# Attention beside a feed-forward block on one core: the bounds' minimum taken once, the ranges compared together, a round's parts summed into C, and another table for the planner

## The chip, the cores and the metric

The kernel runs on one core of one Trainium2 chip. Its time is the device time of one execution, in microseconds (us). Five engines work side by side, each through its own list of instructions in order: TensorE (PE in the profile, its weight loads PEld), VectorE (DVE), ScalarE (ACT), GpSimd (POOL) and SyncE (SP), which here issues nearly all transfers. An instruction that waits holds up everything behind it on its own engine. The kernel before takes 1034.79 us (median of three runs, 1033.28 to 1035.25).

## The reference

One input `x` of 2048 rows by 512 columns goes through two branches, and a gate per row mixes them:

```python
x = A_x
g = _sigmoid((x * gate_w).sum(-1, keepdims=True))
a = _A_ref(x, A_wq, A_wk, A_wv, A_wo)   # attention: 32 heads of 16 columns, one shared k and v
b = _B_ref(x, B_w1, B_w2)               # silu(x @ w1) @ w2, 1792 hidden columns
return g * a + (1 - g) * b
```

Attention is `softmax(q k^T / 4) v` for each of 32 heads over all 2048 keys. That is 32 x 2048 x 2048 exponentials, and all of them are taken on ACT.

## The kernel before

**Rounds and steps.** The queries are cut into 4 chunks `c` of 512 rows and 4 groups `o` of 8 heads; a round is half a group (`rb` 0 or 1), so there are 32 rounds. A round has 16 steps `s`, one for each 128 keys, and a step has two halves `p`. For each half PE makes scores `S` for 128 keys of two heads by 512 queries (L1363, 8 small matmuls, two at 64 rows each of the array's height side by side), and ACT takes the exponential of 128x1024 of them into `P` (L1369). That makes 1024 activations, with two score buffers between PE and ACT. Then the sums over the keys: `pv += P v` (L1467).

**Two ways for a step's sums.** `P` is float32. Either PE multiplies it as it is with `VF` (float32; "native", 16 matmuls in the trace for a step in one piece, or 32 narrower ones for a step in two halves), or DVE first subtracts the upper 16 bits of `P` from it into `L` (L1388), and PE multiplies the upper half and `L` with 16-bit `VP` (8 + 8 matmuls). The second way takes less of PE and one DVE subtraction over 128x2048.

**The end of a round.** When a round's last sums are in, DVE transposes the two accumulators into `T` and `U` (L1282, L1283). GpSimd adds them (L1288), scales six "digits" of v by powers of a quarter into `U` (L1289) and adds the two halves of `T` (L1290). DVE sums the digits (L1304), adds them to their base, column 0 of `T` (L1305), takes the reciprocal of the denominators (L1306) and multiplies into `C` (L1309). After two rounds `turned` transposes `C` and splits it into 16-bit `O` (L1315 to L1318) for the output product. In the last round DVE does GpSimd's part too (`late`).

**The work between.** The feed-forward block (`ffn_h`, `ffn_o`), the q products of later blocks and the output products are fed to PE in small slots of four or eight matmuls between scores (`f_slot`, L1009): four when one product uses half of the array's rows, eight when two products share it. What has not been placed when the rounds are over runs at the end as whole 128-row matmuls (L1013). Results are added to `acc` on DVE (L983) and stored.

**The bound of the scores.** The exponential is taken of scores shifted by a bound computed from |q| and the largest |k| (`q_bound`, then `shift` writes `s1`, which SP stores to `sh` in DRAM through `q_shift`, L516). To know at the end that no bound was too loose, `q_shift` returns `note`: the least entry of `s1`, one DVE reduction for each of the 16 blocks into a column of `um` (L518). The planner queues it as a task of low urgency.

**The check.** When all pieces of weights are split, `chores` take largest absolute values of the operands (L254). When those are done and no block's bound is open, `gather` folds `um` and `mxs` into one row (L815 to L819), SP sends that row to DRAM and `row` brings it back to one partition (L820, L825). `check` compares eleven ranges, three at a time, each with a reduction and two comparisons (L831 to L836); `verdict` writes `flag` (L839 to L841). If it is raised, a second pass computes everything again with measured scales.

**What sets the order.** Nothing is scheduled at run time. While the program is written, a planner keeps a clock for each engine (`pe`, `act`, `dve`, `pool`) and writes the instructions in the order its rules choose: `put(dur, ready, due, f)` queues a DVE task, `serve` takes open tasks by their due time, and the main loop decides between scores, sums and slots. `Way` holds twelve thresholds of these rules, and the table `WAYS` gives new values every eight halves `p`. So a changed duration in a `put`, or another row in the table, moves instructions on every engine.

Of the kernel before, what the change touches and what calls it, by code (L numbers as in the profile page):

```python
# [18 lines left out]
SHIFT = 32.0  # L19
# [19 lines left out]
    *[(0.1, 0.3, 0.2, 4, 1, 4, 4, 8, 9, 2.66, 1, 3)] * 3,  # L39
    (0.1, 0.1, 0.2, 4, 1, 4, 4, 8, 0.5, 2.66, 1, 2),  # L40
    *[(0.1, 0.1, 0.2, 5, 1, 4, 4, 8, 0.5, 2.66, 1, 2)] * 2,
# [3 lines left out]
    *[(0.1, 0.3, 0.2, 4, 1, 4, 4, 8, 9, 2.66, 1, 3)] * 2,  # L45
    (0.1, 0.1, 0.2, 3, 1, 4, 4, 8, 9, 2.66, 1, 3),
    *[(0.1, 0.3, 0.2, 4, 1, 4, 4, 8, 9, 1.5, 1, 3)] * 2,
    (0.1, 0.3, 0.2, 4, 1, 4, 4, 8, 9, 2.66, 1, 3),
    *[(0.1, 0.3, 0.2, 4, 1, 4, 4, 8, 0.2, 1.5, 1, 3)] * 2,
    *[(0.1, 0.3, 0.2, 4, 1, 4, 4, 8, 9, 2.66, 1, 3)] * 2,  # L50
# [6 lines left out]
    *[(0.1, 0.3, 0.2, 5, 1, 4, 4, 8, 9, 2.66, 1, 3)] * 2,  # L57
# [4 lines left out]
    *[(0.6, 0.3, 0.1, 5, 2, 4, 4, 8, 9, 2.66, 1, 2)] * 2,  # L62
# [4 lines left out]
    *[(0.1, 0.3, 0.2, 4, 1, 4, 4, 8, 9, 2.66, 1, 3)] * 2,  # L67
    (0.1, 0.5, 0.2, 4, 1, 4, 4, 8, 0.2, 1.5, 1, 3),
    *[(0.1, 0.1, 0.35, 4, 1, 4, 4, 8, 0.2, 1.5, 1, 3)] * 2,
    (0.1, 0.3, 0.2, 4, 1, 4, 4, 8, 9, 2.66, 1, 3),  # L70
    (0.1, 0.3, 0.2, 3, 1, 4, 4, 8, 0.2, 2.66, 1, 3),
    *[(0.1, 0.3, 0.1, 4, 1, 4, 4, 8, 9, 2.66, 1, 3)] * 2,
    (0.1, 0.3, 0.2, 4, 1, 4, 4, 8, 9, 2.66, 1, 3),
    (0.1, 0.3, 0.35, 4, 1, 4, 4, 8, 0.5, 2.66, 1, 3),
    *[(0.1, 0.3, 0.2, 4, 1, 4, 4, 8, 9, 2.66, 1, 3)] * 2,
# [3 lines left out]
    *[(0.1, 0.3, 0.2, 4, 1, 4, 4, 8, 9, 2.66, 1, 3)] * 3,  # L79
# [5 lines left out]
    *[(0.1, 0.3, 0.2, 4, 1, 4, 4, 8, 9, 2.66, 1, 3)] * 3,  # L85
# [4 lines left out]
    *[(9, 0.1, 0.2, 4, 0, 4, 4, 8, 9, 2.66, 1, 3)] * 3,  # L90
    *[(0.1, 0.3, 0.2, 4, 1, 4, 4, 8, 9, 2.66, 1, 3)] * 4,
# [5 lines left out]
    *[(0.1, 0.3, 0.2, 4, 1, 4, 4, 8, 9, 2.66, 1, 3)] * 2,  # L97
# [6 lines left out]
    *[(9, 0.3, 0.2, 5, 1, 4, 4, 8, 0.2, 2.66, 1, 3)] * 2,  # L104
    (9, 0.5, 0.2, 5, 1, 4, 4, 8, 0.2, 2.66, 2, 3),
    (0.1, 0.3, 0.2, 4, 1, 4, 4, 8, 0.2, 2.66, 1, 3),
    *[(0.1, 0.3, 0.2, 4, 1, 4, 6, 8, 0.2, 1.5, 1, 3)] * 2,
# [10 lines left out]
    *[(0.1, 0.3, 0.2, 5, 1, 5, 4, 8, 9, 2.66, 1, 3)] * 2,  # L118
# [46 lines left out]
def kernel(  # L165
# [168 lines left out]
    for q in qb_:  # L334
        nc.gpsimd.memset(q, 0.0)
# [1308 lines left out]
```

## Time and profile before

| | us |
|---|---|
| median of three runs (range) | 1034.79 (1033.28 to 1035.25) |
| the profiled execution | 1035.51 |
| its span, first to last instruction | 1033.7 |
| PE busy in it | 1015.9 |
| ACT busy | 992.8 |
| DVE busy | 858.3 |
| GpSimd busy | 388.3 |
| first exponential starts | 32.55 |
| last exponential ends | 1010.06 |

The span falls into three stages: a prologue of 32.5 us without exponentials, the loop of 977.5 us, and 23.6 us behind the last exponential. Busy times of PE are modelled from pipelined matmuls, so 98% busy does not mean that PE has nothing to spare. A group's row gives line, engine, operation, tiles, count, busy us, mean ns of one, and the engine's idle time just before them with what ended it.

### The profile page before, as it was taken

The numbers are of one execution on the slowest core, as the hardware profiler recorded it, in microseconds if no ns is written. First come the engines' busy times: TensorE is split into PE (matmuls) and PEld (weight loads), VectorE is DVE, ScalarE is ACT, GpSimd is POOL, SyncE is SP. The second block draws the span as 40 slices with busy tenths as digits, with TensorE's granted clock in tenths as the row PEclk, the third lists the DMA queues.
The fourth block names the chain that finished last, engine by engine and source line by source line (L and its number), as shares of the span: only waits on it lengthen the run. The fifth ranks groups of instructions, "written<-read, shape, count | busy, mean of one in ns | idle before, by whom it ended". The sixth has DMA issues, their size and how long they took to land.

```text
span 1033.7 us, 65235 instructions
## 1 busy us (share of the span) xinstructions
PE 1015.9 (98%) x30746; PEld 569.4 (55%) x30746; DVE 858.3 (83%) x867; ACT 992.8 (96%) x1116; POOL 388.3 (38%) x272
## 2 busy tenths in 40 slices
PE   7999999999999999999999999999999999999997
PEld 5455655555555556555555565555555565555553
DVE  6797988979899957787787887888897988888896
ACT  5899999999999999999999999999999999999990
POOL 2036116235032452524444315344352246383730
PEclk9999999999999999999999999999999999999999
DMA  7321211200000100000000010000000010000001
GB/s 257 90 63 52 65 54 43 63 12 23 12 15 31 32 22 12 12 21 6 22 23 12 22 53 10 17 12 12 23 12 12 9 47 13 12 12 12 5 4 45
DMA packets 23648, 32.92 MB, mean 32 GB/s; under 512 B 4985, under 2 KB 13338, under 8 KB 23370
## 3 DMA queue, kind: packets, MB, share of 16 engines
q1 hardware_dynamic: 22842, 28.49, 9.0%
q8 instruction: 242, 3.96, 1.7%
q14 instruction: 36, 0.29, 0.1%
q0 software_dynamic: 96, 0.10, 0.0%
q10 hardware_dynamic: 432, 0.07, 0.0%
HBM read 20.12 MB, written 8.52 MB: 28 GB/s over the span
## 4 chain that ended last, share of the span: by engine, by line
PE 52%; ACT 37%; issue 6%; DVE 5%; POOL 0%; ACTq 0%; DVEq 0%; POOLq 0%
ACT P L1369 35%; PE pm L1009 18%; PE pv L1467 17%; PE S L1363 13%; ACT e L1023 2%; DVE L L1388 2%; PE pt L449 1%; PE pm L1013 1%; PE pk L551 1%; PE S L1013 1%; DVE acc L983 0%; DVE T L1282 0%; DVE U L1283 0%; DVE w2s L320 0%; PE pq L244 0%
## 5 line engine op out<-in xcount | busy, mean ns | idle before, releaser
L1369 ACT ACTIVATE P<-S 128x1024 f32<-128x1024 f32 x1024 | 957.6, 1096 | 4.7 <-PE S L1363 2.5
L1388 DVE TENSOR_TENSOR L<-P 128x2048 f16<-128x2048 f32 x223 | 532.5, 2400 | 46.5 <-ACT P L1369 45.6
L1363 PE MATMUL S<-qb,KT 50*32 50x512 f16 x8192 | 441.0, 380 | 3.4 <-ACT P L1369 0.8
L1363 PEld LDWEIGHTS <-KT 50*32 50x32 f16 x8192 | 199.0, 89 | 254.3 <-issue 170.1
L1467 PE MATMUL pv<-P,VF 64*32 64x512 f32 (+1 forms) x5696 | 326.3, 511 | 0.0
L1009 PE MATMUL pm<-xs,w1s 64*32 64x512 f16 x5376 | 258.3, 375 | 0.6 <-DVE O L1251 0.6
L1009 PE MATMUL pm<-w2s,H 64*32 64x512 f16 x5088 | 252.2, 375 | 0.2 <-issue 0.2
L1288 POOL TENSOR_TENSOR T<-T,U 128x512 f32<-128x512 f32 x31 | 88.8, 2865 | 260.8 <-DVE U L1283 260.6
L1030 POOL CAST H<-e 128x512 f16<-128x512 f32 x56 | 67.0, 1197 | 251.3 <-DVE e L1028 246.2
L1009 PEld LDWEIGHTS <-w1s 64*32 64x32 f16 x5376 | 114.3, 92 | 47.3 <-issue 7.4
L1009 PEld LDWEIGHTS <-H 64*32 64x32 f16 x5088 | 111.7, 92 | 46.9 <-issue 5.4
L1467 PEld LDWEIGHTS pv<-P,VF 64*32 64x32 f32 x5696 | 114.8, 106 | 32.3 <-issue 4.3
L1031 POOL TENSOR_TENSOR H<-e,H 128x512 f16<-128x512 f32 x56 | 104.8, 1871 | 4.5
L1467 PE MATMUL pv<-P,VP 64*32 64x512 bf16 x1768 | 98.5, 387 | 0.0
L1467 PE MATMUL pv<-L,VP 64*32 64x512 f16 x1768 | 94.6, 374 | 0.2 <-DVE L L1388 0.2
L1009 PE MATMUL pm<-xs,wqs 64*32 64x512 f16 x1152 | 84.9, 375 | 0.1
L1467 PEld LDWEIGHTS <-VP 64*32 64x32 f16 x3536 | 60.8, 93 | 30.0 <-issue 8.5
L1028 DVE SCALAR_TENSOR_TENSOR e<-e,pm 128x512 f32<-128x512 f32 x56 | 38.4, 686 | 41.8 <-ACT e L1023 41.6
L1009 PE MATMUL pm<-wo_s,O 64*32 64x512 f16 x1440 | 66.5, 375 | 0.7 <-DVE acc L983 0.7
L1317 POOL CAST O<-T 128x512 f16<-128x512 f32 x15 | 21.1, 1409 | 67.1 <-DVE T L1315 56.3
L1290 POOL TENSOR_TENSOR T<-T 128x240 f32<-128x240 f32 x31 | 41.5, 1340 | 0.0
L983 DVE SCALAR_TENSOR_TENSOR acc<-pm,g,acc 128x512 f32<-128x512 f32 x43 | 32.1, 746 | 10.9 <-PE pm L1009 10.9
(176 smaller groups left out, 567.6 us busy)
## 6 DMA issues: line engine op xcount, KB each, us to landing
qb<-qd SPq DMA_DIRECT2D x189, 32.0 KB
raw<-in_B_w_dram SPq DMA_DIRECT2D x22, 256.0 KB
xn<-in_A_x_dram SPq DMA_DIRECT2D x8, 512.0 KB
out_dram<-acc SPq DMA_DIRECT2D x16, 256.0 KB
qd<-qx SPq DMA_DIRECT2D x12, 256.0 KB
w1r<-in_B_w_dram SPq DMA_DIRECT2D x2, 512.0 KB
raw<-in_A_wo_dram SPq DMA_DIRECT2D x4, 256.0 KB
qb<-sh SPq DMA_DIRECT2D x62, 2.0 KB
```

The costliest lines, as they stand in the source:

```text
L983: nc.vector.scalar_tensor_tensor(a, po, gate[:, n:n + 1], a, op0=OP.mult, op1=OP.add)
L1009: nc.tensor.matmul(self.bank[32 * m:32 * m + 32], l(i, rows, 32 * m), r(j, rows), start=first, stop=last)
L1028: nc.vector.scalar_tensor_tensor(e, e, 1.0, ph, op0=OP.add, op1=OP.mult)
L1030: nc.gpsimd.tensor_copy(H[:, 0], e)
L1031: nc.gpsimd.tensor_tensor(H[:, 1], e, H[:, 0], op=OP.subtract)
L1288: eng.tensor_tensor(T, T, U, op=OP.add)
L1290: eng.tensor_tensor(T3[:, :, 1:16], T3[:, :, 1:16], T3[:, :, 17:32], op=OP.add)
L1317: eng.tensor_copy(O[:, 0], OT)
L1363: nc.tensor.matmul(sc[32 * m:32 * m + 32, f], KT[b:b + 50, k0:k0 + 32], qtile[i][b:b + 50, j], start=True, stop=True)
L1369: nc.scalar.activation(P[:, 2 * j:2 * j + 2], sc, AF.Exp, scale=scale_of(c, o))
L1388: nc.vector.tensor_tensor(L[s], P, upper(P), op=OP.subtract)
L1467: nc.tensor.matmul(pvs[i][h][32 * j:32 * j + 32, cols], a[r], b[r, j, cols], start=start, stop=rest == n)
```

## The change

Three edits and a table.

First, the minimum of the bounds. `note` and its 16 reductions go; instead a new chore `bounds_back` has SP read the 16 blocks of `sh`, 8 rows of 512 each, from DRAM into the 128 partitions of `least` (a part of `raw0`), and `gather` takes one reduction over them. `open_q` is now popped when the shift itself is done.

Second, the ranges. The limits lie in a constant tile `limits`, filled by nine memsets on GpSimd at the start; `check` is one chore with four reductions and one copy, and `verdict` makes two comparisons over all eleven.

Third, the end of a round. The sum goes into `U` instead of `T`, the sum of the two halves goes straight into `C`, and only then are the digits scaled, in place beside their base, so that one reduction over seven columns gives the whole of column 0. The addition L1305 is gone. The planner's duration for `quotient` falls from 1.08 to 0.80.

Fourth, `WAYS` is another table: 111 of its 128 entries differ from before; the first of them stand below.

```diff
+    limits = consts.tile([1, 2, len(RANGES)], F32)
-    um = consts.tile([64, NO * NCH], F32)
...
     nc.gpsimd.memset(mxs, 0.0)
+    for side in range(2):
+        for n in range(len(RANGES)):
+            if n == 0 or RANGES[n][2 + side] != RANGES[n - 1][2 + side]:
+                nc.gpsimd.memset(limits[:, side, n:], RANGES[n][2 + side])
...
-        n = c * NO + o
-        return lambda: nc.vector.tensor_reduce(um[:, n:n + 1], s1, axis=AX.X, op=OP.min)
...
+        least = raw_[0].bitcast(F16)[:, 512:1024]
+
+        def bounds_back():
+            for c in range(NCH):
+                for o in range(NO):
+                    n = 8 * (c * NO + o)
+                    nc.sync.dma_start(least[n:n + 8], sh[o, c][:, 0])
+
         def gather():
-            nc.vector.tensor_reduce(mr[0:64], um, axis=AX.X, op=OP.min)
-            nc.vector.tensor_scalar(mxs[0:64, M_B:M_B + 1], mr[0:64], -1.0, SHIFT * LAM / ONE, op0=OP.mult, op1=OP.add)
+            nc.vector.tensor_reduce(mr, least, axis=AX.X, op=OP.min)
+            nc.vector.tensor_scalar(mxs[:, M_B:M_B + 1], mr, -1.0, SHIFT * LAM / ONE, op0=OP.mult, op1=OP.add)
...
-            for n in range(n0, min(n0 + 3, len(RANGES))):
-                a, b, lo, hi = RANGES[n]
+            for n, (a, b, _, _) in enumerate(RANGES[:single]):
                 nc.vector.tensor_reduce(g[:, 0, n:n + 1], m1[:, a:b], axis=AX.X, op=OP.max)
-                nc.vector.tensor_scalar(g[:, 1, n:n + 1], g[:, 0, n:n + 1], lo, None, op0=OP.is_lt)
-                nc.vector.tensor_scalar(g[:, 2, n:n + 1], g[:, 0, n:n + 1], hi, None, op0=OP.is_gt)
+            nc.vector.tensor_copy(g[:, 0, single:], m1[:, RANGES[single][0]:])
...
-                note = q_shift(o, c, s1)
+                q_shift(o, c, s1)
+                open_q.pop()
...
-                put(0.67, dve[0] + 0.1, dve[0] + 10, lambda: (note(), open_q.pop()))
...
-                eng.tensor_tensor(T, T, U, op=OP.add)
-                eng.tensor_tensor(z[:, :, 1:1 + DIGITS], T3[:, :, 17:17 + DIGITS], mu[:, :, 1:].to_broadcast([128, 16, DIGITS]), op=OP.mult)
-                eng.tensor_tensor(T3[:, :, 1:16], T3[:, :, 1:16], T3[:, :, 17:32], op=OP.add)
+                eng.tensor_tensor(U, T, U, op=OP.add)
+                eng.tensor_tensor(C[:, :, 1:16], z[:, :, 1:16], z[:, :, 17:32], op=OP.add)
+                eng.tensor_tensor(z[:, :, 1:1 + DIGITS], z[:, :, 17:17 + DIGITS], mu[:, :, 1:].to_broadcast([128, 16, DIGITS]), op=OP.mult)
...
-                nc.vector.tensor_reduce(y.rearrange("p a b -> p (a b)"), z[:, :, 1:1 + DIGITS], axis=AX.X, op=OP.add)
-                nc.vector.tensor_tensor(T3[:, :, 0:1], T3[:, :, 0:1], y, op=OP.add)
-                nc.vector.reciprocal(r, T3[:, :, 16:17])
+                nc.vector.reciprocal(r, z[:, :, 16:17])
+                nc.vector.tensor_reduce(C[:, :, 0:1], z[:, :, 0:1 + DIGITS], axis=AX.X, op=OP.add)
+                nc.vector.tensor_tensor(C, C, r.to_broadcast([128, 16, 16]), op=OP.mult)
...
 WAYS = [
     (0.1, 0.3, 0.2, 4, 1, 4, 4, 8, 9, 2.66, 1, 3),
-    (0.1, 0.3, 0.2, 4, 1, 4, 4, 8, 0.2, 2.66, 2, 3),
+    (0.1, 0.3, 0.2, 4, 1, 4, 4, 8, 0.5, 1.5, 1, 3),
+    (0.1, 0.1, 0.2, 4, 1, 4, 4, 8, 9, 2.66, 1, 3),
...
```

How the order of the first pass moves, counted over whole engines in the two built programs:

| in the first pass | before | changed |
|---|---|---|
| steps summed by way of `L` (16 matmuls) | 221 | 229 |
| native steps in one piece | 226 | 207 |
| native steps in two halves | 65 | 76 |
| subtractions into `L` on DVE | 223 | 232 |
| slots in which two products share the array | 1587 | 1587 |
| slots with one product only | 90 | 114 |
| whole matmuls behind the rounds (`w2s` + `wo_s`) | 36 + 12 | 24 + 12 |
| behind the last scores on PE: sums by 8 matmuls of 16 bits | 5 | 4 |
| ... native steps | 1 | 1 |
| ... slots shared, slots with one product | 10, 12 | 5, 12 |
| DVE instructions of all kinds | 872 | 807 |

The first place is SP where the last block's `s1` is stored, before and changed. `qd` is a block of q in DRAM, `sh` its shift, `qb` the buffer of the next round's q; the change's line numbers are its own.

```order
L392 DMA qb_82<-sh_2_112 1x2x512
L1105 DMA qd_3_113<-qx 128x1024
L516 DMA sh_3_114<-e 4x512 x2
L388 DMA qb_81<-qd_3_89 16x2x512
L389 DMA qb_81<-qd_3_89 16x2x512
L390 DMA qb_81<-qd_3_89 16x2x512
```

```order
L405 DMA qb_82<-sh_2_112 1x2x512
L1123 DMA qd_3_113<-qx 128x1024
L529 DMA sh_3_114<-e 4x512 x2
L829 DMA raw_79<-sh_0_84 8x512
L829 DMA raw_79<-sh_0_92 8x512
L829 DMA raw_79<-sh_0_100 8x512
```

Sixteen reads (L829) now stand between the last store of `sh` and the loads of the next round's q, which follow them.

The second place is DVE from the last shift (L1251, in the change L1269) to `gather` (L815, in the change L833). `e<-pm` of 64x512 is the shift, `acc` an output tile.

```order
L1251 TENSOR_SCALAR e<-pm 64x512
L518 TENSOR_REDUCE um<-e 64x1
L1388 TENSOR_TENSOR L<-P 128x2048
L983 SCALAR_TENSOR_TENSOR acc<-pm,g_65,acc 128x512
L1388 TENSOR_TENSOR L<-P 128x2048
L815 TENSOR_REDUCE raw_79<-um 64x1
```

```order
L1269 TENSOR_SCALAR e<-pm 64x512
L1325 RECIPROCAL rr<-U 128x16
L1326 TENSOR_REDUCE C<-U 128x16
L1327 TENSOR_TENSOR C<-C,rr 128x16x16
L1406 TENSOR_TENSOR L<-P 128x2048
L1333 STREAM_TRANSPOSE T<-C 128x512
L1001 SCALAR_TENSOR_TENSOR acc<-pm,g_65,acc 128x512
L1406 TENSOR_TENSOR L<-P 128x2048 x2
L1046 SCALAR_TENSOR_TENSOR e<-e,pm 128x512
L1406 TENSOR_TENSOR L<-P 128x2048
L1303 STREAM_TRANSPOSE T<-pv_22865 128x512
L1304 STREAM_TRANSPOSE U<-pv_22866 128x512
```

`gather`'s reduction L833 is the next row of the changed order. It stands behind twelve other instructions since the shift, where before it stood behind four.

The third place is the end of DVE's list, from the last reciprocal on: the last `quotient`, `turned`, and the output tiles (`g` of the feed-forward block, `gg` of attention; `S` and `pm` are the banks they lie in).

```order
L1306 RECIPROCAL rr<-T 128x16
L1309 TENSOR_TENSOR C<-T,rr 128x16x16
L983 SCALAR_TENSOR_TENSOR acc<-pm,g_65,acc 128x512
L1315 STREAM_TRANSPOSE T<-C 128x512
L1317 CAST O<-T 128x512
L1318 TENSOR_TENSOR O<-T,O 128x512
L983 SCALAR_TENSOR_TENSOR acc<-S,g_65,acc 128x512 x3
L983 SCALAR_TENSOR_TENSOR acc<-S,gg,acc 128x512
L983 SCALAR_TENSOR_TENSOR acc<-pm,gg,acc 128x512 x2
L983 SCALAR_TENSOR_TENSOR acc<-S,gg,acc 128x512
L983 SCALAR_TENSOR_TENSOR acc<-S,g_65,acc 128x512 x2
```

```order
L1325 RECIPROCAL rr<-U 128x16
L1326 TENSOR_REDUCE C<-U 128x16
L1327 TENSOR_TENSOR C<-C,rr 128x16x16
L1001 SCALAR_TENSOR_TENSOR acc<-pm,g_65,acc 128x512
L1333 STREAM_TRANSPOSE T<-C 128x512
L1335 CAST O<-T 128x512
L1336 TENSOR_TENSOR O<-T,O 128x512
L1001 SCALAR_TENSOR_TENSOR acc<-S,g_65,acc 128x512 x3
L1001 SCALAR_TENSOR_TENSOR acc<-S,gg,acc 128x512
L1001 SCALAR_TENSOR_TENSOR acc<-pm,gg,acc 128x512 x2
L1001 SCALAR_TENSOR_TENSOR acc<-S,gg,acc 128x512
L1001 SCALAR_TENSOR_TENSOR acc<-S,g_65,acc 128x512
```

One output tile fewer is left for the end. On PE it is the tile of twelve whole matmuls out of `w2s`.

More of the change, by code (lines that the diff above doesn't have):

```diff
@@ L660, in first_pass @@
             next(q1)
-            note = shift(0, bank("pk", 2))
+            shift(0, bank("pk", 2))
             step()
@@ L827, in chores, with check @@
         g = raw_[1][0:1, 160:160 + 4 * len(RANGES)].rearrange("p (a b) -> p a b", a=4)
-        def check(n0):
-            if n0 == 0:
-                nc.vector.tensor_reduce(m1, m.rearrange("p (a b) -> p b a", a=4), axis=AX.X, op=OP.max)
-            for n in range(n0, min(n0 + 3, len(RANGES))):
-                a, b, lo, hi = RANGES[n]
+        def check():
+            single = next(n for n in range(len(RANGES)) if all(b - a == 1 for a, b, _, _ in RANGES[n:]))
+            nc.vector.tensor_reduce(m1, m.rearrange("p (a b) -> p b a", a=4), axis=AX.X, op=OP.max)
+            for n, (a, b, _, _) in enumerate(RANGES[:single]):
                 nc.vector.tensor_reduce(g[:, 0, n:n + 1], m1[:, a:b], axis=AX.X, op=OP.max)
-                nc.vector.tensor_scalar(g[:, 1, n:n + 1], g[:, 0, n:n + 1], lo, None, op0=OP.is_lt)
-                nc.vector.tensor_scalar(g[:, 2, n:n + 1], g[:, 0, n:n + 1], hi, None, op0=OP.is_gt)
+            nc.vector.tensor_copy(g[:, 0, single:], m1[:, RANGES[single][0]:])
         def verdict():
+            nc.vector.tensor_tensor(g[:, 1], g[:, 0], limits[:, 0], op=OP.is_lt)
+            nc.vector.tensor_tensor(g[:, 2], g[:, 0], limits[:, 1], op=OP.is_gt)
             nc.vector.tensor_tensor(g[:, 3], g[:, 1], g[:, 2], op=OP.max)
@@ L841, in verdict @@
             nc.vector.tensor_copy(flag, g[:, 0, 0:1])
-        return todo, gather, row, *(lambda n=n: check(n) for n in range(0, len(RANGES), 3)), verdict
+        return todo, bounds_back, gather, row, check, verdict
     def row_maxima(g0, gs, gp, wqs, qsc):
@@ L1272, in norm_a @@
             T, U = wp.tile([128, 512], F32, name="T"), wp.tile([128, 512], F32, name="U")
-            T3, z = (t.rearrange("p (a b) -> p a b", b=32) for t in (T, U))
+            z = U.rearrange("p (a b) -> p a b", b=32)
+            if rb == 0:
+                state["C"] = wp.tile([128, 16, 32], F32, name="C")
+            C = state["C"][:, :, 16 * rb:16 * rb + 16]
             late = i == len(rounds) - 1
@@ L1287, in joined @@
             def joined():
-                eng.tensor_tensor(T, T, U, op=OP.add)
-                eng.tensor_tensor(z[:, :, 1:1 + DIGITS], T3[:, :, 17:17 + DIGITS], mu[:, :, 1:].to_broadcast([128, 16, DIGITS]), op=OP.mult)
-                eng.tensor_tensor(T3[:, :, 1:16], T3[:, :, 1:16], T3[:, :, 17:32], op=OP.add)
+                eng.tensor_tensor(U, T, U, op=OP.add)
+                eng.tensor_tensor(C[:, :, 1:16], z[:, :, 1:16], z[:, :, 17:32], op=OP.add)
+                eng.tensor_tensor(z[:, :, 1:1 + DIGITS], z[:, :, 17:17 + DIGITS], mu[:, :, 1:].to_broadcast([128, 16, DIGITS]), op=OP.mult)
                 if late:
-                    dve[0] += 1.3
-                q = of_norm[0] = put(1.08, dve[0], dve[0], quotient, turns=not late)
+                    dve[0] += 1.2
+                q = of_norm[0] = put(0.80, dve[0], dve[0], quotient, turns=not late)
                 if not late:
```

61 lines of the change are left out of this document (26 added, 35 removed), and 121 rows, old and new, of the table WAYS.

## The prediction

> **What bounds the kernel now.** I read first how busy each engine is over the span, then ACT alone by stages, then who waits for whom, and last the end of the program instruction by instruction. ACT by stages (columns: stretch, its length, busy us with the number of instructions, clock, transfers):
>
> ```profile
> core 0: us, ACT busy (x), PEclk, DMA share, GB/s
> 32.55:204.00 171.45, 168.54 (x186) 1.00 0.22 63
> 204.00:404.00 200.00, 199.92 (x223) 1.00 0.07 20
> ...
> 604.00:785.00 181.00, 181.00 (x203) 1.00 0.07 18
> 785.00:1010.06 225.06, 223.62 (x249) 1.00 0.05 14
> ```
>
> From the first exponential to the last ACT hardly ever rests: 2.9 us of idle time in the first 171 us, 1.4 us in the last 225, next to nothing between. So within the loop ACT sets the pace, and its work is the same in both kernels: 1024 exponentials and 56 tanh.
>
> ```profile
> 640.09 0.79 ACT L1023 ACTIVATE e<-pm 128x512 f32<-128x512 f32 x1
> 640.57 20.48 ACT L1369 ACTIVATE P<-S 128x1024 f32<-128x1024 f32 x22
> ...
> L1369 ACT ACTIVATE P<-S 128x1024 f32<-128x1024 f32 x1024 | 957.6, 1096 | 4.7 <-PE S L1363 2.5 <-DMA qb<-qd 0.3 <-ACT P L1369 0.2
> ...
> PEld L1363 <- issue: 170.1, 709, 0.7
> ```
>
> Here 22 exponentials take 20.48 us; with one's own 1.2 us at the end taken off, they come 0.918 us apart. A tanh puts 0.48 us between (640.09 to 640.57). At that pace the loop lasts 1024 x 0.918 + 56 x 0.48 = 966.9 us. It lasts 1010.06 - 32.55 = 977.5. The 10.6 us between are the slip: scores that came late. They are all that the loop can still give, and a good part is the start, where PE has nothing done ahead. PE is called 98% busy, but its loads for scores stand idle 170 us in 709 pieces, which is PE waiting for ACT to give a score buffer back. The loop is ACT's; PE is late only in places. Behind the loop nothing runs on ACT, and the end belongs to PE and DVE.
>
> ```profile
> 1008.52 0.41 PE L1363 MATMUL S<-qb,KT 50*32 50x512 f16 x8
> 1008.74 0.41 PE L1467 MATMUL pv<-L,VP 64*32 64x512 f16 x8
> 1008.96 1.48 PE L1009 MATMUL pm<-w2s,H 64*32 64x512 f16 x48
> 1010.25 0.42 PE L1467 MATMUL pv<-P,VP 64*32 64x512 bf16 x8
> 1010.48 0.41 PE L1467 MATMUL pv<-L,VP 64*32 64x512 f16 x8
> 1010.69 1.05 PE L1467 MATMUL pv<-P,VF 64*32 64x512 f32 x16
> 1011.55 1.05 PE L1009 MATMUL pm<-w2s,H 64*32 64x512 f16 x32
> ...
> 1012.64 0.40 PE L1467 MATMUL pv<-L,VP 64*32 64x512 f16 x8
> 1013.21 2.77 PE L1009 MATMUL pm<-w2s,H 64*32 64x512 f16 x48 [0.16 <-issue]
> 1015.91 4.06 PE L1013 MATMUL S<-w2s,H 128*128 128x512 f16 x18
> ```
>
> Starts give prices, since matmuls are pipelined: scores 0.22 us, eight sums of 16 bits 0.22 (10.25 to 10.48 to 10.69), a native step 0.86 (10.69 to 11.55), six shared slots 1.29 or 0.215 each, twelve slots of one product 2.70 (13.21 to 15.91), and a whole matmul (4.06 - 0.38) / 17 = 0.2165.
>
> **The change, part by part.** *The end.* Behind the last scores PE has before: 0.22 + 5 x 0.22 + 0.86 + 10 x 0.215 = 4.33 us, and 0.36 of waiting until 1013.21. In the changed order one group of 16-bit sums and five shared slots fewer stand there: 0.22 + 4 x 0.22 + 0.86 + 5 x 0.215 = 3.04. That is 1.29 us less before the last round closes. Then both have 2.70 of single slots, and the change has 36 whole matmuls for 48: 12 x 0.2165 = 2.60 less. PE ends 3.89 us earlier against the last exponential. DVE must follow:
>
> ```profile
> 1013.34 0.71 DVE L1282 STREAM_TRANSPOSE T<-pv 128x512 f32<-128x512 f32 x1
> 1016.18 0.19 DVE L1305 TENSOR_TENSOR T<-T,yy 128x16 f32<-128x16 f32 x1
> 1018.75 0.69 DVE L1318 TENSOR_TENSOR O<-T,O 128x512 f16<-128x512 f32 x1
> 1019.36 1.41 DVE L983 SCALAR_TENSOR_TENSOR acc<-S,g,acc 128x512 f32<-128x512 f32 x2
> 1026.83 0.75 DVE L983 SCALAR_TENSOR_TENSOR acc<-S,g,acc 128x512 f32<-128x512 f32 x1 [0.54 <-PE S L1013]
> 1027.61 0.85 SPq L986 DMA_DIRECT2D out_dram<-acc  x1
> ```
>
> From the last sums (1012.64 + 0.40 = 1013.04) to `O` it takes 6.4 us; without L1305 some 6.2. Eight output tiles follow at 0.70: 5.6 us, so DVE could end 11.8 us behind the last sums. PE needs 0.2 + 2.70 + 36 x 0.2165 = 10.7, some 0.3 for banks, and the last tile's 0.85: 11.8 as well. Before it was 1027.58 - 1013.04 = 14.5. So 2.7 of it at most arrives, and since two equal chains meet I take 2.5: with the 1.29, **3.8 us off the end**. Bounds: 3.0 if the banks hold PE up once more, 4.3 if the wait of 0.36 goes too. Stores and leaving stay as they are.
>
> *The loop on PE.* Eight steps go from native to split: 8 x (0.44 - 0.86) = -3.4 us, 0.2 of that back since one group leaves the end. Slots with one product rise from 90 to 114, all in the loop: 24 x 0.2165 = +5.2. Five shared slots come in from the end: +1.1. Sum: +3.1 us of PE work in the loop. By the same prices the loop held 1023 scores, 1577 shared and 78 single slots, 24 whole matmuls, 218 split steps and 290 native ones: 221 + 339 + 17 + 5 + 96 + 249 = 927 of 977.5 us. Room for 3.1 is there, under ACT's pace; it costs at nothing where PE waits for ACT, and all of 5.2 if every new single slot delays a score. I take 0 and keep -4.6 (the slip of the loop's later part going) to +5.2.
>
> *DVE.* Five groups of before:
>
> ```profile
> L518 DVE TENSOR_REDUCE um<-e 64x1 f32<-64x512 f16 x12 | 8.1, 672 | 0.1
> L1305 DVE TENSOR_TENSOR T<-T,yy 128x16 f32<-128x16 f32 x32 | 11.1, 346 | 1.1
> L835 DVE TENSOR_SCALAR raw<-raw 1x1 f32<-1x1 f32 x11 | 1.6, 141 | 0.4
> L836 DVE TENSOR_SCALAR raw<-raw 1x1 f32<-1x1 f32 x11 | 1.4, 131 | 0.0
> L1388 DVE TENSOR_TENSOR L<-P 128x2048 f16<-128x2048 f32 x223 | 532.5, 2400 | 46.5 <-ACT P L1369 45.6 <-PE pv L1467 0.5
> ```
>
> Sixteen reductions of 0.67 go (10.7) and one comes. The 32 additions go (11.1), and a reduction over seven columns for six adds under 1. Of the ranges' comparisons 3.0 goes, and some 0.4 comes. That is 23 us less, and nine more subtractions of 2.40 take 21.6 of it back. DVE ends as loaded as before, 858 us, and this edit alone is worth nothing: L1388 stands idle 45.6 us waiting for exponentials, so DVE follows ACT. What it buys is the eight split steps. GpSimd's three operations are the same in another order; it is busy 388 us of the span, and its sums were waited for by nothing on PE.
>
> *The reads.* SP issues sixteen more transfers, ahead of the q of round 24, and DVE's `gather` now waits for their landing. How fast SP issues:
>
> ```profile
> 734.71 0.34 SPq L388 DMA_DIRECT2D qb<-qd  x1
> ...
> 736.04 0.54 SPq L392 DMA_DIRECT2D qb<-sh  x1
> 736.68 0.55 SPq L820 DMA_DIRECT2D md<-raw  x1
> 738.31 0.23 SPq L825 DMA_DIRECT2D raw<-md  x1
> 763.14 0.33 SPq L388 DMA_DIRECT2D qb<-qd  x1
> ...
> qb<-qd POOLq DMA_DIRECT2D x3, 32.0 KB, 2.0
> ```
>
> A transfer takes SP 0.34 to 0.54 us: 5.4 to 8.6 for sixteen, and the last lands about 2.0 later (the row of GpSimd's queue; 1.63 passed between sending `md` and the read that needed it). That is 7 to 11 us after the last shift. Between that shift and `gather` the changed order has on DVE four subtractions (9.6), three of a quotient (1.0), three transposes (2.1), an output tile and a tanh's gate (1.4): 14.1 us. They hide the reads, with 3 us to spare at worst; uncovered they would stall every DVE task behind. Behind the reads on SP are loads needed a round later. The flag is read on SP soon after `raw<-md`, and its wait lasts until `verdict`, which in the changed order stands before round 23 closes: about 760, ahead of the next loads (763.14). Nothing. The Trainium skill (DMA: Bandwidth & Descriptors, Rules for kernel authors and Anatomy of one DMA) speaks against such reads: small transfers should be merged, each pays about 2.0 us however small. If each paid in turn, the sixteen would take 32 us; the row shows issues 0.4 to 0.6 apart, which do not wait for landings.
>
> *The start.* Nine memsets on GpSimd come ahead of the first iota.
>
> ```profile
> 3.08 0.30 POOL L340 MEMSET mu<- 128x1 f32 x7
> 3.68 0.23 DVE L347 TENSOR_SCALAR ident<-jp 128x128 f32<-128x128 f32 x1 [3.68 <-POOL jp L344]
> 4.78 0.32 PEld L449 LDWEIGHTS pt<-ident,xn 128*128 128x128 f32 x2 [4.78 <-DVE rm L368]
> ```
>
> Seven small ones take 0.30 us, so nine take 0.4, and 0.9 if each takes its own 0.1. The identity was ready at 3.91 and the first transpose started at 4.78: nothing to 0.1 us.
>
> The sum: 1035.51 - 3.8 + 0 = 1031.7 in the terms of the profiled execution. That execution is 0.7 above the median of the runs, so against the median 1034.79 the forecast is **1031.0 us**.
>
> **The rivals.** (a) *The loop gives the gain back.* The slip arises where PE is late with a score though it has room on the whole, and the change adds single slots and steps in halves. If half of the 24 single slots delay a score, the loop loses 2.6: 1033.6, no change; with all of them 1036.2. For it: eleven more steps in two halves, and a last stretch where ACT already idles 1.4 us. Against it: 47 us of PE's room, and no idle in 604 to 785.
>
> (b) *Slower: the reads hold DVE.* If the sixteen reads land one after another at 2.0 us, `gather` waits 32 + 0.6 - 14.1 = 18.5 us at the close of round 22. PE has exponentials of four steps in store (4 x 1.84 = 7.4 us); then sums, scores and ACT stop, for 11 us: 1034.8 - 3.8 + 11 = 1042. It decides from 1.7 us apiece; below that the store and the gain at the end cover it. Against it are the rows of SP above. By the skill's fixed price in turn, this is the result.
>
> (c) *The loop gains too.* With eight fewer native steps of 0.86 in front of scores, the slip could fall by 4: 1027. For it: 2.9 of the idle time lies in the first 171 us, where DVE had the 16 reductions and the weights. Against it: the start of the loop has the same order in round 0.
>
> (d) *The flag rises* and the second pass runs, over 900 us more. The values read back are those that were reduced before, so under 1 in 100.
>
> **How the numbers follow.** The forecast 58 in 100, with 1029.0 to 1032.7 as its own range; (c) 10; (a) 21 as no change and 5 as worse; (b) and (d) 6. A change of 0.2%, 2.1 us, is about what a measurement here can tell from none. Faster by that: 58 + 10 = 0.68; within it 0.21; slower 5 + 6 = 0.11. The range 1028.0 to 1035.5 takes in (a) but for its end, and the better part of (c).
>
> **What would show it.** Right: ACT's window from its first to its last exponential again 976 to 979 us; the stretch behind it 19.4 to 20.6 us for 23.6; 36 whole matmuls; DVE still near 858; no stall at L833. Wrong: a wait of DVE for a transfer near 735 us (b); more idle time of ACT than 4.7 us with PE's scores as its releaser (a); a stretch behind the loop above 21 us, with PE waiting for `acc`, would fell the term of the end.

## The result, and the profile after

The changed kernel takes 1031.68 us (median of 13 runs, 1030.47 to 1033.03), the kernel before on the same chip 1034.14 us (13 runs, 1032.77 to 1035.29). The ratio is 0.9977, with a 95% interval from 0.9968 to 0.9986: 2.5 us or 0.23% less, and the interval leaves out no change. In two more sets of runs the ratio was 0.9978 and 0.9966. The profiled execution of the changed kernel took 1032.32 us, with a span of 1030.4.

In the changed kernel's lines the exponential stands at L1387, the subtraction into `L` at L1406, scores at L1381, sums at L1485, slots and whole matmuls at L1027 and L1031, and the output tiles' additions at L1001. First the row of the page with each engine's busy time, its share of the span and its instructions:

```profile
PE 1012.3 (98%) x31006; PEld 575.8 (56%) x31006; DVE 862.4 (84%) x802; ACT 993.2 (96%) x1116; POOL 396.2 (38%) x281
```

Then ACT alone by stages (stretch, its length, busy us with the number of instructions, clock, transfers):

```profile
33.39:204.00 170.61, 169.14 (x187) 1.00 0.20 64
204.00:404.00 200.00, 199.68 (x222) 1.00 0.07 21
404.00:604.00 200.00, 199.45 (x222) 1.00 0.06 20
604.00:785.00 181.00, 180.29 (x202) 1.00 0.06 16
785.00:1010.10 225.10, 224.67 (x251) 1.00 0.05 14
```

ACT is as full as it was. Its idle time is less in the first stage (1.5 us for 2.9) and in the last (0.4 for 1.4), and some lies now in the stages between (1.6 for 0.3). The loop lasts 1010.10 - 33.39 = 976.7 us for 977.5. The groups that the prediction's terms rest on (busy us, mean ns of one, idle time before):

```profile
L1387 ACT ACTIVATE P<-S 128x1024 f32<-128x1024 f32 x1024 | 956.6, 1093 | 3.5 <-PE S L1381 1.7 <-ACT P L1387 0.2
L1406 DVE TENSOR_TENSOR L<-P 128x2048 f16<-128x2048 f32 x232 | 555.9, 2407 | 45.5 <-ACT P L1387 45.0
L1326 DVE TENSOR_REDUCE C<-U 128x16 f32<-128x112 f32 x32 | 6.9, 215 | 0.3
L833 DVE TENSOR_REDUCE raw<-raw 128x1 f32<-128x512 f16 x1 | 0.6, 634 | 0.0
```

DVE is no less busy than before (862.4 us for 858.3), with 65 instructions fewer: the nine added subtractions fill what was saved. L833, the reduction over the bounds read back, waited for nothing. PE behind the last exponential, in order of time (start, us, instructions; in brackets the idle time ahead and what ended it):

```profile
1011.21 0.45 PE L1485 MATMUL pv<-L,VP 64*32 64x512 f16 x8
1011.82 2.77 PE L1027 MATMUL pm<-w2s,H 64*32 64x512 f16 x48 [0.16 <-issue]
1014.53 2.76 PE L1031 MATMUL S<-w2s,H 128*128 128x512 f16 x12
1018.45 1.46 PE L1031 MATMUL S<-w2s,H 128*128 128x512 f16 x6 [1.16 <-DVE acc L1001]
```

Before, PE went on behind its first 18 whole matmuls in one piece with this row:

```profile
1020.16 1.46 PE L1013 MATMUL S<-w2s,H 128*128 128x512 f16 x6 [0.19 <-DVE acc L983]
```

And DVE in the same stretch, with the change:

```profile
1011.72 0.72 DVE L1303 STREAM_TRANSPOSE T<-pv 128x512 f32<-128x512 f32 x1
...
1017.04 0.69 DVE L1336 TENSOR_TENSOR O<-T,O 128x512 f16<-128x512 f32 x1
1017.65 1.40 DVE L1001 SCALAR_TENSOR_TENSOR acc<-S,g,acc 128x512 f32<-128x512 f32 x2
...
1023.83 0.75 DVE L1001 SCALAR_TENSOR_TENSOR acc<-S,g,acc 128x512 f32<-128x512 f32 x1 [0.50 <-PE S L1031]
```

The stretch from the last exponential to the end of the span fell from 23.6 to 20.3 us. PE has 12 whole matmuls in one piece where it had 18, and then stands 1.16 us (0.19 before) until DVE has added the first output tile that shares PSUM space with the next one. The first exponential started 0.83 us later, at 33.39 us; the experiments show below that this is not the change's doing.

### The profile page after: what moved, and what is told of

Same layout as the page of the kernel before. It is cut to its first block, busy times and chain, and to the rows that moved or that the text cites. A ratio compares the mean times of both kernels' runs of the same rounds, so it can differ in the third digit from the quotient of the medians.

```text
span 1030.4 us, 65694 instructions
## 1 busy us (share of the span) xinstructions
PE 1012.3 (98%) x31006; PEld 575.8 (56%) x31006; DVE 862.4 (84%) x802; ACT 993.2 (96%) x1116; POOL 396.2 (38%) x281
## 4 chain that ended last, share of the span: by engine, by line
PE 62%; ACT 23%; DVE 8%; issue 4%; DMA 1%; POOL 0%; SPq 0%; ACTq 0%; DVEq 0%
PE pm L1027 22%; ACT P L1387 22%; PE pv L1485 21%; PE S L1381 15%; DVE L L1406 4%; ACT e L1041 1%; PE pt L462 1%; PE pm L1031 1%; DMA xn<-in_A_x_dram 1%; PE pk L562 1%; DVE e L1046 0%; PE S L1031 0%; DVE acc L1001 0%; DMA raw<-in_B_w_dram 0%; DVE U L1304 0%
## 5 line engine op out<-in xcount | busy, mean ns | idle before, releaser
L1387 ACT ACTIVATE P<-S 128x1024 f32<-128x1024 f32 x1024 | 956.6, 1093 | 3.5 <-PE S L1381 1.7
L1406 DVE TENSOR_TENSOR L<-P 128x2048 f16<-128x2048 f32 x232 | 555.9, 2407 | 45.5 <-ACT P L1387 45.0
L1381 PE MATMUL S<-qb,KT 50*32 50x512 f16 x8192 | 435.9, 380 | 2.4 <-DVE KT L582 0.5
L1381 PEld LDWEIGHTS <-KT 50*32 50x32 f16 x8192 | 194.9, 89 | 240.3 <-issue 154.3
L1485 PE MATMUL pv<-P,VF 64*32 64x512 f32 (+1 forms) x5744 | 317.7, 498 | 0.0
L1027 PE MATMUL pm<-w2s,H 64*32 64x512 f16 x5184 | 261.3, 375 | 0.2 <-issue 0.2
L1027 PE MATMUL pm<-xs,w1s 64*32 64x512 f16 x5376 | 250.9, 375 | 0.7 <-DVE e L1046 0.4
L1309 POOL TENSOR_TENSOR U<-T,U 128x512 f32<-128x512 f32 x31 | 81.2, 2618 | 302.8 <-DVE U L1304 302.8
L1027 PEld LDWEIGHTS <-H 64*32 64x32 f16 x5184 | 115.3, 92 | 41.9 <-issue 3.2
L1027 PEld LDWEIGHTS <-w1s 64*32 64x32 f16 x5376 | 109.6, 92 | 50.6 <-issue 8.1
L1485 PEld LDWEIGHTS pv<-P,VF 64*32 64x32 f32 x5744 | 114.2, 106 | 35.5 <-issue 5.7
L1049 POOL TENSOR_TENSOR H<-e,H 128x512 f16<-128x512 f32 x56 | 113.6, 2029 | 4.5
L1485 PE MATMUL pv<-P,VP 64*32 64x512 bf16 x1832 | 100.9, 387 | 0.2 <-DVE U L1304 0.2
L1485 PE MATMUL pv<-L,VP 64*32 64x512 f16 x1832 | 97.2, 374 | 0.6 <-DVE L L1406 0.4
L1027 PE MATMUL pm<-xs,wqs 64*32 64x512 f16 x1152 | 84.7, 375 | 0.0
L1485 PEld LDWEIGHTS <-VP 64*32 64x32 f16 x3664 | 63.2, 92 | 30.9 <-issue 9.9
L1027 PE MATMUL pm<-wo_s,O 64*32 64x512 f16 x1440 | 66.3, 375 | 0.0
L1001 DVE SCALAR_TENSOR_TENSOR acc<-pm,g,acc 128x512 f32<-128x512 f32 x44 | 32.9, 747 | 17.5 <-PE pm L1027 17.2
L1310 POOL TENSOR_TENSOR C<-U 128x240 f32<-128x240 f32 x31 | 43.3, 1398 | 2.4
L1311 POOL TENSOR_TENSOR U<-U,mu 128x96 f32<-128x96 f32 x31 | 42.8, 1382 | 2.4
```

What stands on the lines that cost most here:

```text
L1001: nc.vector.scalar_tensor_tensor(a, po, gate[:, n:n + 1], a, op0=OP.mult, op1=OP.add)
L1027: nc.tensor.matmul(self.bank[32 * m:32 * m + 32], l(i, rows, 32 * m), r(j, rows), start=first, stop=last)
L1049: nc.gpsimd.tensor_tensor(H[:, 1], e, H[:, 0], op=OP.subtract)
L1309: eng.tensor_tensor(U, T, U, op=OP.add)
L1310: eng.tensor_tensor(C[:, :, 1:16], z[:, :, 1:16], z[:, :, 17:32], op=OP.add)
L1311: eng.tensor_tensor(z[:, :, 1:1 + DIGITS], z[:, :, 17:17 + DIGITS], mu[:, :, 1:].to_broadcast([128, 16, DIGITS]), op=OP.mult)
```

## The experiments

In what follows a time stands beside that of the kernel before from the same chip. Chips differ, so kernels from different sets of runs are compared by their ratios to the kernel before; those of one set also by their medians. "End" is the stretch from the last exponential's end to the end of the span, "loop" that from the first exponential's start to the last one's end.

**The table alone, and the code alone.** The kernel before with the new table, and the changed code with the old table:

```diff
# e1: kernel before
-WAYS = (old rows)
+WAYS = (new rows)
# e2: changed kernel
-WAYS = (new rows)
+WAYS = (old rows)
```

> The kernel before with the new table alone. Its order leaves 96 whole matmuls behind the rounds (48 before, 36 in the change) and takes 217 subtractions into L. Theory (the loop is ACT's, the end is PE's list behind the last scores): the loop from first to last exponential stays at 975 to 979 us, the end grows from 23.6 by 48 x 0.2165 = 10.4, and the time is about 1044. Rival (the table by itself makes the loop better, and the code beside it little): 1034 or less.

> The changed code with the old table. Its order leaves 168 whole matmuls behind the rounds and takes 220 subtractions into L. Theory: loop 975 to 979 us, the end 23.6 + 120 x 0.2165 = 49.6, time about 1060, though DVE has all of its savings. Rival (the work taken off DVE is what makes the kernel faster, whatever the table): 1030 to 1034.

Measured: 1057.26 us, ratio 1.0225 (1.0207 to 1.0243), and 1063.43 us, ratio 1.0285 (1.0266 to 1.0303). Each half of the change alone is over 2% slower. The end of e1 on PE:

```profile
1035.78 9.23 PE L1022 MATMUL S<-w2s,H 128*128 128x512 f16 x42
1044.85 2.75 PE L1022 MATMUL pm<-w2s,H 128*128 128x512 f16 x12
1047.43 1.46 PE L1022 MATMUL S<-w2s,H 128*128 128x512 f16 x6
```

And of e2:

```profile
1029.40 7.93 PE L1022 MATMUL S<-xs,w1s 128*128 128x512 f16 x36
...
1042.36 9.23 PE L1022 MATMUL S<-w2s,H 128*128 128x512 f16 x42
```

What the plan could not place in the loop runs behind it: 96 whole matmuls in e1, 168 in e2, against 48 and 36 in the two kernels. The last exponential of e1 ends at 1021.11 and its end takes 34.1 us, 10.5 more than before; 48 x 0.2165 = 10.4. That of e2 ends at 1012.57, its end takes 49.3 us, 29.0 more than the changed kernel's; 132 x 0.2165 = 28.6. So the price of a whole matmul holds where many are added, and it explains most of e2. The rest of e2 is its loop, 981.0 us long, 3.5 more than before and outside the 975 to 979 expected. In e1 the price does not suffice: the expectation missed by 13 us, since the loop itself became 989.9 us long, 12.4 more. There the two engines wait for each other by turns. ACT's exponentials in the view by groups:

```profile
L1378 ACT ACTIVATE P<-S 128x1024 f32<-128x1024 f32 x1024 | 959.9, 1088 | 15.3 <-PE S L1372 13.3
```

And a row of PE's waits (us in total, times, longest):

```profile
PE S L1372 <- ACT P L1378: 9.3, 23, 1.0
```

ACT waits 13.3 us for scores where it waited 2.5, and PE 9.3 us for score buffers where it waited 0.8. In e2 it is 7.3 and 12.1. We read this as orders that do not fit the engines' real pace. Which thresholds do it was not tried, so the cause of the longer loops is argued and not shown. What follows: neither half has a worth of its own that could be added to the other's.

**Twelve whole matmuls put back.** The changed kernel, with the first two whole tiles of six multiplied twice; the order is the same otherwise:

```diff
+                twice = late_tiles[0] < 2 and o.n == 6
+                late_tiles[0] += twice
+                for _ in range(1 + twice):
                     for n in range(o.n):
                         o.whole(n, n == 0, n == o.n - 1)
```

> The changed kernel, with the first two whole tiles of six matmuls behind the rounds issued twice (12 whole matmuls more, the same output). In the changed profile PE waits 1.16 us for an output tile's eviction there. If PE's list alone set the end: + 12 x 0.2165 = 2.6, 1034.3. If two chains meet, as the changed profile shows: 2.6 less the wait of 1.16 that they fill, + 1.4, 1033.1. If DVE's evictions alone set the end: no change, 1031.7.

Measured: 1032.25 us (before 1033.56), ratio 0.9988 (0.9979 to 0.9997). Against the changed kernel's 0.9977 that is 1.1 us more (the two intervals just overlap), for 2.6 us of work on PE. PE behind the single slots:

```profile
1013.41 6.65 PE L1031 MATMUL S<-w2s,H 128*128 128x512 f16 x30
1019.89 0.81 PE L1031 MATMUL S<-wo_s,O 128*128 128x512 f16 x3
```

The wait of 1.16 us ahead of the third tile is gone: the added work stands in it. The end is 1030.4 - 1008.98 = 21.4 us, 1.1 over the changed kernel's, and the filled wait is 1.16 of the rest. Of the three expectations that of two chains that meet (1.4 us) comes nearest; PE alone would have been 2.6, DVE alone nothing.

**DVE's saving given back.** The changed kernel, with the 32 additions and the reductions of the bounds put back on DVE as dummies (15 reductions in its profile), outside the planner's clocks:

```diff
+                nc.vector.tensor_reduce(spare[0:64, 0:1], s1, axis=AX.X, op=OP.min)
...
+                nc.vector.tensor_tensor(spare[:, 0:16], spare[:, 16:32], spare[:, 32:48], op=OP.add)
```

> The changed kernel in its own order, with DVE work of the kind that went put back as idle work that nothing reads: an addition of 128x16 in each of 32 quotients (0.35 us each, 11 us) and a reduction of 64x512 behind each of 14 shifts (0.67 each, 9.4 us); the planner does not know of it. Theory (DVE follows ACT in the loop, and its savings pay only as steps that go by way of L): 0 to + 0.5, at most 1032.2, with DVE some 20 us busier. Rival (the savings on DVE are the gain): + 2 to + 3, about 1034.

Measured: 1032.2 us (before 1033.56), ratio 0.9985 (0.9976 to 0.9993), 0.8 us over the changed kernel's ratio, with overlapping intervals: a little above the 0 to 0.5 expected, and far from the rival's 2 to 3. Busy times, then ACT early in the loop:

```profile
PE 1013.8 (98%) x31006; PEld 577.6 (56%) x31006; DVE 877.6 (85%) x849; ACT 993.8 (96%) x1116; POOL 387.9 (38%) x282
```

```profile
68.57 1.02 ACT L1391 ACTIVATE P<-S 128x1024 f32<-128x1024 f32 x1 [1.16 <-PE S L1385]
70.28 1.02 ACT L1391 ACTIVATE P<-S 128x1024 f32<-128x1024 f32 x1 [0.68 <-DVE U L1307]
72.08 4.00 ACT L1391 ACTIVATE P<-S 128x1024 f32<-128x1024 f32 x4 [0.78 <-PE S L1385]
```

15.2 us more of DVE's busy time cost less than one by the medians. In the profiled execution, which at 1033.45 us is 1.2 above the median, the cost is in one place, at the close of the first round, where ACT loses 2.6 us ahead of three of its steps. Without them its loop, 980.3 us, would be as long as the changed kernel's. That the dummies cause these waits is likely, since one of them ends with DVE's transpose into `U`, but it was not tested by itself. DVE's load is worth little, as the prediction has it.

**The changed kernel again, and three single edits.** The first of the four is the control. The others: another order of PSUM spaces for the whole tiles; the reads issued only when `gather` needs them; the nine fills put behind the first pass.

```diff
# e6: in spaces(), the loop over the two-bank tiles' halves f
-                yield pM.tile([128, 512], F32, name="pm")
-                yield pM.tile([128, 512], F32, name="pm")
+                    if f == 0:
+                        yield pM.tile([128, 512], F32, name="pm")
+                        yield pM.tile([128, 512], F32, name="pm")
# e7
-        return todo, bounds_back, gather, row, check, verdict
+        return todo, lambda: None, lambda: (bounds_back(), gather()), row, check, verdict
# e8: the loop of nine memsets into limits moved
```

> The changed kernel as it is, again, so that the next three stand beside it on one chip. Both theories: 1031 to 1032.3 us, ratio to the kernel before 0.997 to 0.999. Its first exponential was late by 0.83 us in its first profile (33.39 against 32.55 us); if that is the spread of the first input transfer and not the change, it now starts anywhere from 30.9 to 33.4 us.

> The changed kernel, with another order in which the whole tiles of the end take their PSUM space: the two tiles of a bank each come before the second two-bank tile, so that no whole tile waits for another that shares its PSUM tile. Theory (TensorE's wait of 1.16 us for the eviction of an output tile lies on the end's path): the wait goes, the end behind the last exponential falls from 20.3 to about 19.2 us, and the time is 0.8 to 1.2 us under the changed kernel. Rival (the wait only moves to the next tile, or VectorE's evictions set the end): within 0.3 us of the changed kernel.

> The changed kernel, with the 16 reads issued just ahead of the reduction that needs them, with no other VectorE work put between: VectorE stands until they have landed. Theory (the reads take 7 to 11 us and are hidden in the changed kernel by the work between): a wait of 7 to 11 us for a transfer shows at the reduction, and the time rises by 2 to 6 us, since VectorE is some 85% busy there and can win back part of it. Rival (reads that wait for nothing, and land in about 2 us): a wait under 3 us, and the time within 1 us of the changed kernel.

> The changed kernel, with GpSimd's nine fills of the table of limits moved from the start of the program to behind the first pass, where they are needed later still. Theory (the fills cost the start nothing to 0.1 us): the time within 0.2 us of the changed kernel, and the first exponential anywhere from 30.9 to 33.4 us, as in the others. Rival (the fills made the first exponential late by 0.83 us): the time 0.5 to 0.9 us under the changed kernel, and a first exponential before 32.6 us.

| | us | ratio to before (95%) | first exponential | loop | end |
|---|---|---|---|---|---|
| e5, changed kernel | 1031.42 | 0.9978 (0.9968 to 0.9988) | 31.25 | 978.1 | 20.2 |
| e6, spaces | 1030.62 | 0.9964 (0.9950 to 0.9977) | 31.07 | 978.3 | 19.7 |
| e7, reads at once | 1036.88 | 1.0022 (1.0011 to 1.0034) | 32.95 | 981.6 | 20.3 |
| e8, fills late | 1031.33 | 0.9972 (0.9960 to 0.9984) | 30.91 | 978.6 | 20.2 |

e8 is the changed kernel to within 0.1 us, so the fills cost nothing. And the control, with the fills in place, starts its first exponential at 31.25 us: the 33.39 of the first profile is the spread of the start.

In e6 the long wait is gone, and a shorter one stands later:

```profile
1016.38 1.46 PE L1031 MATMUL pm<-w2s,H 128*128 128x512 f16 x6
1017.67 0.81 PE L1031 MATMUL pm<-wo_s,O 128*128 128x512 f16 x3
1018.32 1.46 PE L1031 MATMUL S<-wo_s,O 128*128 128x512 f16 x6
1020.34 0.81 PE L1031 MATMUL S<-wo_s,O 128*128 128x512 f16 x3 [0.56 <-DVE acc L1001]
1020.99 1.45 PE L1031 MATMUL S<-w2s,H 128*128 128x512 f16 x6
```

The end is 19.7 us, not the 19.2 expected: it shrinks by 0.5 us, the median time by 0.8. Half of the wait lay on the path, and the rest of it moved to the next space.

e7 gives the price of the reads. The timeline of SP, DVE, PE and ACT around `gather` in e7:

```profile
739.22 5.50 SPq L829 DMA_DIRECT2D raw<-sh  x16
...
746.28 0.69 DVE L833 TENSOR_REDUCE raw<-raw 128x1 f32<-128x512 f16 x1 [4.95 <-DMA raw<-sh]
...
747.79 0.65 DVE L1046 SCALAR_TENSOR_TENSOR e<-e,pm 128x512 f32<-128x512 f32 x1
...
748.49 0.41 PE L1027 MATMUL pm<-xs,w1s 64*32 64x512 f16 x8 [3.29 <-DVE e L1046]
...
749.25 3.83 ACT L1387 ACTIVATE P<-S 128x1024 f32<-128x1024 f32 x4 [3.50 <-PE S L1381]
```

SP and DVE at the same place in the changed kernel:

```profile
726.40 5.40 SPq L829 DMA_DIRECT2D raw<-sh  x16
...
740.52 0.63 DVE L833 TENSOR_REDUCE raw<-raw 128x1 f32<-128x512 f16 x1
```

Sixteen reads take SP 5.5 us to issue, and DVE goes on 7.06 us after the first (739.22 to 746.28). The changed kernel leaves 14.1 us between the two (726.40 to 740.52), so they were hidden with 7 us to spare. The stall is under the 7 us expected, 4.95, because DVE reached `gather` 2.1 us after the first read had gone out; the cost of 3.5 us in the loop, and 5.5 by the medians, lies in the range of 2 to 6. Where it went is told by the last two rows of e7: PE stood 3.29 us for a tanh's gate `e`, which was queued on DVE behind the stalled reduction, and ACT for the scores behind that.

**The kernel before again, and the spaces in it.** A second profile of the kernel before, and that kernel with e6's order of spaces:

```diff
# e10: kernel before, spaces()
-                yield pM.tile([128, 512], F32, name="pm")
-                yield pM.tile([128, 512], F32, name="pm")
+                    if f == 0:
+                        yield pM.tile([128, 512], F32, name="pm")
+                        yield pM.tile([128, 512], F32, name="pm")
```

> The kernel before as it is, profiled once more, for the spread of its start and of its loop. Theory (the first input transfer's spread moves the first exponential in every kernel, and the loop makes up a part of it): the first exponential anywhere from 30.9 to 33.4 us, the loop 977 to 979.5 us long, the end behind it again 23.65 us to within 0.4. Rival (the change itself shortened the loop by 0.8 us): a loop of 978.5 us or more at an early start, against 978.1 to 978.6 in the changed kernel's profiles with an early start.

> The kernel before with the same other order of PSUM spaces as in e6. Theory (in the kernel before, 18 whole matmuls stand ahead of the wait for the first eviction behind the round's close, and only 0.19 us of wait was left; the changed kernel lost six of them there, which became the wait of 1.16 us): the time within 0.6 us of the kernel before, and the last eviction at most 0.6 us earlier against the last exponential. Rival (the order of spaces is worth about the same anywhere): 0.8 us or more off.

e9 took 1034.05 us beside 1033.61 of the same kernel (ratio 1.0004, 0.9995 to 1.0014): this is what no change looks like. Its first exponential starts at 31.13 us, its end takes 23.4 us, and its loop only 976.6, less than either theory said. With the change the loop had been 0.8 us shorter; with this profile it is longer. e10 took 1033.22 us, ratio 0.9996 (0.9987 to 1.0006): nothing gained that can be told from noise, and the last output tile's addition ends 17.6 us behind the last exponential as in e9 (17.5). The medians alone would not decide this: e10 lies 0.8 us under e9, as far as e6 under e5. The profiles do: e6 moves the last addition from 14.5 us behind the last exponential to 13.9, e10 does not move it. So in these two kernels the order of spaces is worth something only where too little whole work stands ahead of the wait.

**The other order of spaces once more, beside the changed kernel.** No new edit.

> The kernel of e6 once more, beside the changed kernel on one chip, since the intervals of the two overlapped. Theory (the end behind the last exponential is 0.5 us shorter, by e6's profile 19.65 against 20.16 us): ratio 0.996 to 0.9975, 0.4 to 1.0 us under the changed kernel, and 19.5 to 19.8 us behind the last exponential again. Rival (the 0.8 us of e6 were mostly chance): within 0.3 us of the changed kernel.

> The changed kernel a third time, the partner of the run with the other order of spaces. Ratio 0.997 to 0.9985. Its loop tells which of its two earlier profiles is the usual one: 978.0 us or more from the first exponential to the last if the change made the loop some 1 us longer than the 976.6 to 977.5 of the kernel before, under 977.3 if the loops are alike.

e11: 1030.09 us, ratio 0.9960 (0.9947 to 0.9974), end 19.5 us. e12: 1030.62 us, ratio 0.9966 (0.9952 to 0.9979), just under its range, end 20.2 us. Its loop of 977.3 us lies at the edge of one of the two cases set for it and decides little. The version with the other order was 0.8 and 0.5 us under the changed kernel on two chips, and its end 0.5 and 0.7 us shorter. The last addition ends 13.9 us behind the last exponential in both of its profiles, and 14.5 us in all three of the changed kernel. The intervals of the times overlap, but times and profiles agree, so this is likely the fastest of the kernels tried.

## Why the prediction came out so

**The total.** Forecast 1031.0 us within 1028.0 to 1035.5; measured 1031.68. Its likeliest case, a gain at the end and a loop that stays, is what happened. Its size was too large: 3.8 us forecast, 2.5 measured. That the total came within 0.7 us is in part luck: half of the difference did not show in it, since the median of three runs from which it was counted, 1034.79, stood 0.65 above the median of thirteen.

**The end: right in its mechanism, mis-sized by half a microsecond.** Of the 3.8 us, 3.3 arrived: 3.0 by the last addition, the rest with the last stores. The first part, 1.29 us less on PE before the last round closes, came in full: the last sums started 2.58 us behind the last exponential (1012.64 - 1010.06), and now 1.11 us (1011.21 - 1010.10), which is 1.47 less. The second, 2.5 us between the last sums and the last addition, was too large: that stretch fell from 14.5 to 12.9 us (1011.66 to 1024.58), by 1.6. The step that failed is "some 0.3 for banks": PE waited 1.16. The sum had counted DVE's and PE's chains each for itself and found both 11.8 us long, but they are coupled in the middle. From the last sums DVE needs 6.1 us to `O` and 0.7 more for the first whole tile's addition, and only then does PE get the space for its third tile. Of the twelve removed matmuls six stood ahead of this point (18 before, 12 after), where PE had been only 0.19 us early. Of their 1.30 us, 0.97 became wait (1.16 for 0.19); the rest arrived because DVE's chain to `O` is shorter too, 6.1 us for 6.4. The prediction had named this case: 3.0 us "if the banks hold PE up once more" was its lower bound, and it forecast 3.8. e3 shows the coupling from the one side (over half of the work put there is free, and the wait vanishes), e6 from the other (spaces given otherwise, the wait halves and the end follows), e10 by the kernel before, in which the same order of spaces gains nothing.

**The loop: forecast to stay, and it stayed to within what these profiles can tell.** The changed kernel's three profiles have loops of 976.7, 978.1 and 977.3 us, the kernel before's two 977.5 and 976.6. With the kernels whose edits lie wholly outside the loop, seven profiles of the changed order average 977.8 and three of the order before 976.9. That leans to 0.9 us given back, and with the end's 3.3 it would make about the 2.5 that the clock shows. The two groups overlap (976.7 and 977.3 in the one, 977.5 in the other). Among the profiles with an early first exponential they do not, with 977.3 to 978.6 six times against 976.6 twice, but two are few, so it isn't settled. If the 0.9 us is real, it is not rival (a)'s late scores. Within the loop ACT stands idle 4.2 to 4.6 us in the three profiles of the order before and 3.5 to 4.5 in the seven of the changed order. What is larger is its busy time: 972.2 to 972.9 us there and 973.2 to 974.1 here, for the same 1080 instructions. Why they take 1.2 us more is open. Rival (c), a loop that gains 4 us, is out.

One reading under that forecast was wrong. The 170 us ahead of the score loads were taken for PE waiting for ACT's buffers, but the row puts them to "issue", which is time in which the engine waited for nothing that the profile shows. PE's waits for ACT's score buffers come to 0.8 us in the whole profile before, and 0.4 after. So how much room PE had in the loop isn't shown. Two prices were also a little off, without effect: 24 single slots at 2.70 / 12 are 5.4 us and not 5.2, and 1023 scores at 0.22 are 225 us and not 221.

**DVE.** Right: 862.4 us for 858.3, and e4 prices another 15.2 us of load at under one.

**The reads.** Right: 7 to 11 us forecast, 7.1 measured, behind 14.1 us, the very figure that the prediction had counted. That it agrees to the tenth is chance: it runs from the first read, 0.7 us behind the shift, and has 1.4 us in it in which DVE stood idle. Rival (b), sixteen reads in turn at 2.0 us each, is out: they are through in 7.1 us, at 0.34 us an issue. Here the Trainium skill (DMA: Bandwidth & Descriptors, Anatomy of one DMA) states a fixed part of about 2.0 us for each transfer that GpSimd issues. On SP's queue the trace shows something like it once for the batch (1.6 us from SP's last issue done, 744.72, to DVE's start), not for each of the sixteen. But one step of that rival's price was wrong the other way. It gave PE "exponentials of four steps in store (4 x 1.84 = 7.4 us)", so that a stall under that would cost nothing; e7's stall of 4.95 us cost ACT 3.5. The store holds for sums only. PE takes its instructions in order, and the next of them that needed DVE was no sum but a slot that waited for a gate.

**The start.** Right: nothing for the fills. The first profile had 0.83 us against it, and a single pair of profiles would have charged that to the change; over all fourteen profiles the first exponential starts from 30.9 to 33.4 us, at 32.55 and 31.13 with the kernel before, and at 33.39, 31.25 and 30.91 with the changed one.

**The test set beforehand.** "A stretch behind the loop above 21 us, with PE waiting for `acc`, would fell the term of the end": the stretch was 20.3 us, and PE did wait for `acc`. So the term stood, and the wait that the sentence names was what it lacked.

## What to carry to other kernels

Where two engines finish a program together, don't add up each one's work and take the longer: look for the point in the middle at which one needs the other, and count what stands ahead of it on both sides. Work removed ahead of such a point becomes a wait, and a new order of buffers may then be worth what it was not worth before. And a table tuned for one order of instructions belongs to that order: each half of this change alone cost 24 to 30 us, and together they gained 2.5.

## What the runs showed of the hardware that was not expected

The first exponential's start moved by 2.5 us between executions, from 30.9 to 33.4 us, and by as much with the changed kernel alone (33.39, 31.25 and 30.91). The expectations took this for the spread of the first input transfer, and the traces show that as a part only: PE's first weight load for a transpose began at 4.78 us both in the first profile of the kernel before and in e7, which start late (32.55 and 32.95 us), at 5.43 in the first profile of the changed kernel (33.39), and at 4.67 to 5.08 in the eleven that start early. Two of the late ones then wait 0.77 us (the changed kernel's first) and 1.46 us (e7) for further rows of `x`. The larger part is PE's pace. In the three profiles with a late start the first three q products start 0.43 us apart, at 10.9 to 12.5 us; in e9 and e8, which start early, they start 0.21 to 0.22 apart. When the long run of k products begins, the first profile of the kernel before is already 1.43 us behind e9 (20.42 and 18.99 us), which is all that its first exponential is late by. The profile gives a granted clock of 1.00 in these stretches all the same, and why PE kept the slower pace longer in some executions is open. So a difference under some 2.5 us between two profiles' spans says little here; the stretches inside them have to be compared one by one.
